# First tokens projected without their LayerNorm, the factors multiplied in behind: an attention and MLP kernel on one Trainium2 core

## The chip, the cores and the metric

The kernel runs on one core of one Trainium2 chip. The metric is the device time of one execution in microseconds; the time of a kernel is the median of its runs.

## What is computed

One input `x` (2048 tokens of 512) goes through a LayerNorm without parameters, and the result `xn` feeds two branches that meet at the end:

```python
def _layernorm(x, axis=-1, eps=1e-5):
    m = jnp.mean(x, axis=axis, keepdims=True)
    v = jnp.var(x, axis=axis, keepdims=True)
    return (x - m) / jnp.sqrt(v + eps)

xn = _layernorm(x)
# attention: 32 heads of 128, 2048 cached keys and values, no mask
q = (xn @ wq).reshape(B, Sq, H, Dh).transpose(0, 2, 1, 3)
p = softmax(einsum("bhqd,bhkd->bhqk", q, k_cache) * Dh ** -0.5)
s = einsum("bhqk,bhkd->bhqd", p, v_cache).transpose(...).reshape(B, Sq, H * Dh) @ wo
# MLP: 512 -> 512 (gelu), shifted by tokens in four column groups, -> 512; then 512 -> 1792 -> 512
x1 = xn + shift(gelu(layernorm(xn) @ w1)) @ w2
g = silu(x1 + gelu(layernorm(x1) @ w3) @ w4)
out = x + s * g
```

Inputs are bf16.

## The kernel before

Attention is cut into 128 units. A unit is one head and 512 queries; units go by groups of four heads, and within a group by the four blocks of 512 queries, so units 0 to 3 are the first 512 tokens with heads 0 to 3, units 4 to 7 the next 512 tokens. A unit has 8 steps (`SPU`), 1024 in all; the loop over `n` in the main function writes out the order of the work by hand, step by step, and `pin` keeps each engine's instructions in that order. A step does, on TensorE, two score matmuls (`s_slot`: 128 keys by 512 queries each, into one of two PSUM buffers `ps_s`), one exp of both on ScalarE, and the two PV matmuls of an earlier step (`pv_slot`, into a bank of `psO`, which has two). The distance between a step's scores and its PV is the lag: `LAG` at first, one more behind each entry of `STEPS`. So before the change the lag is 5 up to step 35, 6 up to 39, 7 up to 43, 8 up to 47, and in the long run 10 to 12.

Everything else is woven in between. VectorE adds up the exps of a unit (`add_first`, `add_next`, `fold`, all of the tile `acc`); the row sums come out of matmuls with a column of ones for units 0 to 3 (`sums`) and out of a DMA transpose for the later ones; the reciprocals go to DRAM and come back broadcast over the partitions (`recip`, `bcast`: DMAs on SP's queue), and `norm` multiplies them into the PV result, which frees its PSUM bank. The query projection of a unit is four matmuls (`q_mm`) and a copy (`q_copy`). MLP chunks are dealt out evenly from step 42 on, into the PSUM bank with the tag `xm`; the other bank of the pool `psX`, tag `xa`, serves queries, sums and output projection in turn.

LayerNorm of x goes by tiles of 128 tokens: `ln1_load`, `ln1_stats` (`bn_stats`, `bn_aggr` on VectorE, the reciprocal root as two small GpSimd instructions), `ln1_apply` (VectorE), `ln1_turn` (a DMA transpose into `xnT`). The tuple `tokens` gives the steps at which tiles 4 to 15 do so. Tiles 0 to 3 are handled before step 0, by `first_stats` and `first_tokens`: normalise, transpose on TensorE against an identity matrix, copy to `xnT`, project unit 0's query in four pieces of 128 tokens. Units 1 to 3 get their queries at steps 1, 3 and 5, four matmuls at a time. Before all that, `warm_up` runs 48 small matmuls on the identity. Loads are issued on three queues: SP (`nc.sync`), ScalarE's (`nc.scalar`) and GpSimd's (`nc.gpsimd`); `load_k`, `load_v` and `load_w` fetch a head's K (transposing, in four pieces), V (two halves) and query weights.

Helpers record every matmul at one line (L122), so groups are told apart by their tiles: `ps_s` scores, `ps_o` PV, `ps_q` queries, `ps_m` MLP, `ps_wo` output projection, `ps_sum` row sums.

## Time and profile before

| | us |
|---|---|
| median of 3 runs | 1249.71 |
| lowest and highest | 1249.54, 1253.06 |
| profiled execution | 1248.59 |
| its span, first to last instruction | 1246.8 |
| TensorE busy | 1239.2 |
| ScalarE busy | 1129.5 |
| VectorE busy | 1115.2 |
| GpSimd busy | 171.3 |

The profile is of one execution. A row of its timeline gives the start, the length, the engine, the line, the operation with its output and inputs, the number of instructions merged, and in brackets the idle time of the engine ahead of it and what ended that. A row of a group gives the number of instructions behind an x, the busy time, the mean of one in ns, and the idle time ahead of them. PE is TensorE's matmuls and PEld its weight loads, DVE VectorE, ACT ScalarE, POOL GpSimd, SP SyncE; a trailing q is the engine's DMA queue. Matmuls overlap, so the sum of their durations is more than the time they take: their pace is read from starts.

### The profile page before, as it was taken

Reading aid. Unit: us, or ns where it says so; the run is one execution under the profiler, and the core shown is the slowest. Engines: PE = TensorE matmul, PEld = TensorE weight load, DVE = VectorE, ACT = ScalarE, POOL = GpSimd, SP = SyncE. Lnnn points to the kernel's source line nnn. Section 1 sums busy time; section 2 is a strip of 40 time slices with the busy share of each in tenths; the row PEclk is TensorE's granted clock in tenths of the full one; section 3 lists DMA queues with packets and bytes.
Section 4 is the critical chain, followed back from the end, with each engine's and each line's share of the span. In section 5 each row is a group of like instructions: output and inputs, shape, how many; then the busy total and the mean of one; then the engine's idle time right before and its main releaser. Section 6 shows DMA issues by size and latency. Waiting matters only on the chain.

```text
span 1246.8 us, 16616 instructions
## 1 busy us (share of the span) xinstructions
PE 1239.2 (99%) x5808; PEld 596.4 (48%) x5808; DVE 1115.2 (89%) x1518; ACT 1129.5 (91%) x1285; POOL 171.3 (14%) x299
## 2 busy tenths in 40 slices
PE   8999999999999999999999999999999999999998
PEld 5444444444444444444444444444444444444444
DVE  7999999999899988899989889899888999888998
ACT  8999999888999888899998889998888999988992
POOL 5563003432111000000100000010000000000110
PEclk9999999999999999999999999999999999999999
DMA  9556473565734545243573345633345233653453
GB/s 198 126 111 104 88 154 77 129 130 114 153 67 101 114 98 120 55 88 73 108 155 85 68 76 106 136 79 83 81 105 119 56 89 66 130 136 77 106 149 106
DMA packets 248404, 131.42 MB, mean 105 GB/s; under 512 B 200000, under 2 KB 224960, under 8 KB 248320
## 3 DMA queue, kind: packets, MB, share of 16 engines
q1 hardware_dynamic: 238752, 103.94, 41.1%
q0 software_dynamic: 8992, 25.96, 8.0%
q8 instruction: 45, 0.74, 0.3%
q10 hardware_dynamic: 576, 0.46, 0.1%
q14 instruction: 39, 0.32, 0.1%
HBM read 83.62 MB, written 8.13 MB: 74 GB/s over the span
## 4 chain that ended last, share of the span: by engine, by line
PE 93%; DVE 3%; DMA 2%; ACT 1%; issue 0%; SPq 0%; DVEq 0%
PE ps_s L122 34%; PE ps_o L122 33%; PE ps_m L122 9%; PE ps_wo L122 8%; PE ps_q L122 8%; DMA rb<-dr 1%; DVE acc L224 1%; ACT pT L213 1%; DMA dr<-rc 0%; DVE acc L219 0%; DMA accT<-acc 0%; DVE qT L199 0%; DVE sm L266 0%; DVE acc L228 0%; DVE oT L293 0%
## 5 line engine op out<-in xcount | busy, mean ns | idle before, releaser
L213 ACT ACTIVATE pT<-ps_s 128x1024 bf16<-128x1024 f32 x1024 | 1022.1, 1029 | 90.7 <-PE ps_s L122 76.3
L122 PE MATMUL ps_s<-qT,kT 128*128 128x512 bf16 x2048 | 608.8, 379 | 0.8 <-ACT pT L213 0.5
L122 PE MATMUL ps_o<-pT,vb 128*128 128x512 bf16 x2048 | 607.4, 379 | 0.4 <-DVE oT L300 0.4
L122 PEld LDWEIGHTS <-kT 128*128 128x128 bf16 x2048 | 231.7, 113 | 228.8 <-issue 6.0
L224 DVE TENSOR_TENSOR acc<-acc,pT 128x2048 bf16<-128x2048 bf16 x256 | 308.9, 1207 | 7.3 <-ACT pT L213 6.6
L122 PEld LDWEIGHTS <-vb 128*128 128x128 bf16 x2048 | 200.2, 98 | 226.0 <-issue 0.7
L219 DVE TENSOR_TENSOR acc<-pT 128x2048 bf16<-128x2048 bf16 x128 | 156.2, 1221 | 30.9 <-ACT pT L213 30.5
L122 PE MATMUL ps_q<-xnT,wq_h 128*128 128x512 bf16 (+1 forms) x524 | 152.8, 374 | 0.6 <-ACT xnT L477 0.4
L293 DVE TENSOR_TENSOR oT<-ps_o,rb 128x512 bf16<-128x512 f32 x122 | 130.8, 1072 | 9.5 <-DMA rb<-dr 9.4
L122 PE MATMUL ps_wo<-wo_h,oT 128*128 128x512 bf16 (+1 forms) x460 | 135.1, 377 | 0.0
L379 DVE TENSOR_TENSOR s_acc<-ps_wo,s_acc 128x512 f32<-128x512 f32 x96 | 66.0, 688 | 42.6 <-PE ps_wo L122 42.4
L228 DVE TENSOR_TENSOR acc<-acc 128x1024 bf16<-128x1024 bf16 x128 | 87.5, 683 | 0.9
L266 DVE TENSOR_REDUCE sm<-accT 128x4 f32<-128x512 bf16 x122 | 83.0, 680 | 1.1 <-DMA accT<-acc 1.0
L199 DVE CAST qT<-ps_q 128x512 bf16<-128x512 f32 x109 | 75.0, 688 | 7.9 <-PE ps_q L122 6.9
L122 PEld LDWEIGHTS <-wq_h 128*128 128x128 bf16 x524 | 50.8, 98 | 60.8 <-issue 1.0
L122 PE MATMUL ps_m<-w_sb,h2T 128*128 128x512 bf16 x224 | 77.1, 379 | 0.5 <-DVE xr L700 0.5
L122 PE MATMUL ps_m<-xn2T,w_sb 128*128 128x512 bf16 x224 | 77.1, 379 | 0.0
L682 POOL DMA_DIRECT2D w_sb<-in_B_w_dram x28 | 21.2, 756 | 372.3 <-PE ps_m L122 325.3
L122 PEld LDWEIGHTS <-oT 128*128 128x128 bf16 x468 | 45.7, 98 | 54.1
L710 POOL DMA_DIRECT2D g_d<-xr x16 | 8.8, 548 | 438.3 <-DVE xr L708 438.3
L229 DVE TENSOR_TENSOR acc<-acc 128x512 bf16<-128x512 bf16 x128 | 54.4, 425 | 4.4
L514 DVE SCALAR_TENSOR_TENSOR sq<-sq,pre 128x1024 bf16<-128x1024 bf16 x36 | 44.0, 1222 | 4.7 <-ACT sq L510 4.6
(98 smaller groups left out, 627.9 us busy)
## 6 DMA issues: line engine op xcount, KB each, us to landing
rb<-dr SPq DMA_DIRECT2D x127, 256.0 KB, 3.9
vb<-in_A_v_cache_dram SPq DMA_DIRECT2D x60, 256.0 KB, 3.4
w_sb<-in_B_w_dram POOLq DMA_DIRECT2D x28, 256.0 KB, 3.6
wo_h<-in_A_wo_dram SPq DMA_DIRECT2D x32, 128.0 KB, 2.8
wq_h<-in_A_wq_dram SPq DMA_DIRECT2D x28, 128.0 KB, 2.9
kT<-in_A_k_cache_dram SPq DMA_TRANSPOSE x128, 3.4
dr<-rc SPq DMA_DIRECT2D x128, 2.0 KB, 1.7
xr<-in_A_x_dram POOLq DMA_DIRECT2D x16, 128.0 KB, 2.5
```

The lines of the kernel that those rows point to most:

```text
L122: pin(nc.tensor.matmul(out=out, lhsT=lhsT, rhs=rhs, start=start, stop=stop))
L199: pin(nc.vector.tensor_copy(out=qT[:], in_=st[u].pop("psq")[:]))
L213: pin(nc.scalar.activation(out=s["pT"][-1][:, jj:jj + 2, :], in_=sps[:], func=ACT.Exp, scale=SCALE))
L219: pin(nc.vector.tensor_tensor(out=s["acc"][:], in0=s["pT"][0][:], in1=s["pT"][1][:], op=ALU.add))
L224: pin(nc.vector.tensor_tensor(out=a[:], in0=a[:], in1=st[u]["pT"][i][:], op=ALU.add))
L228: pin(nc.vector.tensor_tensor(out=a[:, 0:2, :], in0=a[:, 0:2, :], in1=a[:, 2:4, :], op=ALU.add))
L229: pin(nc.vector.tensor_tensor(out=a[:, 0, :], in0=a[:, 0, :], in1=a[:, 1, :], op=ALU.add))
L266: pin(nc.vector.tensor_reduce(out=sm[:], in_=s.pop("at")[:], axis=mybir.AxisListType.X, op=ALU.add))
L293: pin(nc.vector.tensor_tensor(out=oTs[(g, qt)][:, hh, :].rearrange(f, j=4), in0=s["o"].rearrange(f, j=4), in1=s["rb"].rearrange("x (p j) - ...
L379: pin(nc.vector.tensor_tensor(out=sa, in0=ps[:], in1=sa, op=ALU.add))
L514: pin(nc.vector.scalar_tensor_tensor(out=sq[:].rearrange(f2), in0=sq[:].rearrange(f2), scalar=1.0, in1=pre[:].rearrange(f2), op0=ALU.add, ...
L682: pin(nc.gpsimd.dma_start(out=w[:], in_=w3_v[:, :, fc * P:(fc + 2) * P]))
```

## The change

The change has three parts.

First, the four tiles of the first 512 tokens are no longer normalised before they are projected. `first_tokens` transposes the raw x on TensorE (`turn`, `back`) into a tile `xT`. The mean is taken out on the side of the weights: `middle` multiplies a head's query weights with a matrix of -1/512, copies the result (`cs`) to SBUF, and GpSimd adds it to the weights in one instruction per head (`wc`), so that the projection of raw x by `wc` is that of x less its mean. The reciprocal roots of the variances come behind: `factor` spreads them over the partitions with fp32 matmuls against a diagonal matrix (`rsA` broadcast, `diag`), and `q_scale` multiplies them into the projected queries on VectorE. `first_stats` takes all four tiles on VectorE and one root of four columns on GpSimd. The query matmuls of units 1 to 3 become single ones and pairs: two ahead of step 0, two each at steps 0, 1, 2 and 15, one each at 9 and 12 (`raw_q`, `raw_fill`). Tiles 0 to 3 are still normalised for the MLP, tile 0 ahead of step 0 and the others at steps 0 and 1, and are transposed by DMA at steps 34, 40, 46 and 52. Tiles 8 to 15 have other steps in `tokens`.

Second, the third unit (`u == 2`) gathers its PV in the bank `xm`, and the normalisations of units 0 to 3 move from steps 18, 26, 34, 42 to 26, 34, 38, 42; broadcasts 1 and 3 have other SBUF buffers. The queries of units 4 to 6 use the bank `xa`, those of 5 and 6 in two pairs instead of four singles.

Third, the lag starts at 3 and grows to 4, 5 and 6 behind steps 15, 23 and 32, and is as before from step 36 on. The warm-up has 23 matmuls on the -1/512 matrix, with 4 more ahead of the query projection. x tiles 0 to 3 are all loaded on SP's queue, the first two query weights on ScalarE's; unit 0's V halves stand between its K pieces; the loads of tiles 4 to 7 move ahead, and V of the second head moves from ahead of step 0 to steps 2 and 4, that of the third from steps 3 and 4 to 7 and 8, all on GpSimd's queue.

```diff
-    LAG = 5
+    LAG = 3
-    WARM = 48
+    WARM = 23
+    FILL = 4
...
-    STEPS = (36, 40, 44, 48, 49, 150, 158)
+    STEPS = (15, 23, 32, 40, 44, 48, 49, 150, 158)
...
+            s["o"] = (psX.tile([P, 512], FP32, tag="xm", name="ps_o") if u == 2 else
+                      psO.tile([P, 512], FP32, name="ps_o"))
...
     def first_stats():
...
+        ve = smp.tile([P, 4], FP32, tag="rc", name="ve4")
+        for a in range(2):
+            bns = [smp.tile([P, nc.vector.BN_STATS_DIM], FP32, name="bn") for _ in range(2)]
+            for j in range(2):
+                pin(nc.vector.bn_stats(out=bns[j][:], in_=ln[2 * a + j][:]))
+            for j in range(2):
+                pin(nc.vector.bn_aggr(out=mvA[:, 2 * a + j, :], in_=bns[j][:]))
+        pin(nc.vector.tensor_scalar(
+            out=ve[:], in0=mvA[:, :, 1], scalar1=EPS, scalar2=None, op0=ALU.add))
+        return lambda: pin(nc.gpsimd.tensor_tensor(
+            out=rsA[:], in0=ve[:], in1=nhalf[:, 0:1].to_broadcast([P, 4]), op=ALU.pow))
...
+    def q_raw(h, dcs, ps, cs=slice(0, 512)):
+        for dc in dcs:
+            mm(ps[:, cs], raw[h][:, dc, :], raw["xT"][:, dc, cs], dc == 0, dc == DC - 1)
+
+    def q_scale(h, ps, rb, cs=slice(0, 512)):
+        if h not in st:
+            st[h] = dict(qT=qtp.tile([P, 512], BF16, name="qT"))
+        pin(nc.vector.tensor_tensor(out=st[h]["qT"][:, cs], in0=ps, in1=rb, op=ALU.mult))
...
     def first_tokens():
...
+        def factor(i):
+            rp_ = psO.tile([P, 256], FP32, tag="ps_o", name="ps_r")
+            for j in range(2):
+                t = 2 * i + j
+                mm(rp_[:, j * P:(j + 1) * P], rsA[:, t:t + 1].to_broadcast([P, P]), diag[:], True, True)
+            return rp_
+
+        tok = lambda t: slice(t * P, (t + 1) * P)
+        roots = first_stats()
+        for t in range(2):
+            turn(t)
+            back(t)
+        middle((0,), psX.tile([P, P], FP32, tag="xa", name="ps_c"))
+        for t in range(2, 4):
+            turn(t)
+            back(t)
+        roots()
+        middle((1,), psO.tile([P, P], FP32, tag="ps_o", name="ps_c"))
+        warm_up(FILL, psX.tile([P, P], FP32, tag="xm", name="ps_w"))
+        ps = [psX.tile([P, 512], FP32, tag=tag, name="ps_q") for tag in ("xa", "xm")]
+        for i in range(2):
+            for t in (2 * i, 2 * i + 1):
+                q_raw(0, range(DC), ps[i], tok(t))
+            pin(nc.scalar.activation(out=qs[:, halves[i]], in_=ps[i][:, halves[i]], func=ACT.Identity))
+        rps = [factor(i) for i in range(2)]
+        ln1_apply(0)
+        for i in range(2):
+            q_scale(0, rps[i][:], qs[:, halves[i]], halves[i])
+        middle((2,), psX.tile([P, P], FP32, tag="xm", name="ps_c"))
+        for i in range(2):
+            pin(nc.scalar.activation(out=rsb[:, halves[i]], in_=rps[i][:], func=ACT.Identity))
+
+    def middle(hs, cp, eng=None):
+        c = slice(hs[0] * P, hs[0] * P + P)
+        for h in hs:
+            for dc in range(DC):
+                mm(cp[:], raw["mean"][:], wqs[h][:, dc, :], dc == 0, dc == DC - 1)
...
+        for h in hs:
+            wide(h)
+            pin(nc.gpsimd.tensor_tensor(
+                out=raw[h], in0=wqs[h][:], in1=raw["cs"][:, h * P:(h + 1) * P].unsqueeze(1).broadcast_to([P, DC, P]),
+                op=ALU.add))
...
-    for t, eng in enumerate([nc.sync, nc.scalar, nc.sync, nc.scalar]):
+    for h in range(2):
+        load_w(h, nc.scalar)
+    for t, eng in enumerate([nc.sync] * 4):
         ln1_load(t, eng)
+    for i in range(2):
+        load_k(0, (2 * i, 2 * i + 1))
+        load_v(0, (i,))
+    raw_q = {-1: [(1, 0), (1, 1)], 0: [(1, 2), (1, 3)], 1: [(2, 0), (2, 1)], 2: [(2, 2), (2, 3)],
+             9: [(3, 0)], 12: [(3, 1)], 15: [(3, 2), (3, 3)]}
...
     first_tokens()
-    load_v(1, (0, 1), nc.gpsimd)
...
-        at(3 + i, lambda i=i: load_v(2, (i,), nc.gpsimd))
+        at(2 + 2 * i, lambda i=i: load_v(1, (i,), nc.gpsimd))
+        at(7 + i, lambda i=i: load_v(2, (i,), nc.gpsimd))
...
+    norms = {26: 0, 34: 1, 38: 2, 42: 3}
...
+    scales = {2: 1, 5: 2, 15: 3}
+    raw_fill(-1)
     for n in range(NS):
...
-        if u == 0 and p in (1, 3, 5):
-            q_mm(1 + p // 2, range(DC))
-        if u == 0 and p in (2, 4, 6):
-            q_copy(p // 2)
+        if n == 2:
+            middle((3,), psO.tile([P, P], FP32, tag="ps_o", name="ps_c"), nc.vector)
+        raw_fill(n)
+        if n in scales:
+            h = scales[n]
+            q_scale(h, raw["ps", h][:], raw["rb"][:])
+        if n in (0, 1):
+            for t in (2 * n, 2 * n + 1)[n == 0:]:
+                ln1_apply(t)
+        if n in (34, 40, 46, 52):
+            ln1_turn((n - 34) // 6)
...
+        if n in norms:
+            normed(norms[n])
-        if p == 2 and u >= 2 and not turned(u - 2):
+        if p == 2 and u > HG + 1 and not turned(u - 2):
             normed(u - 2)
```

More of the change, by code (lines that the diff above doesn't have):

```diff
@@ L496, in first_tokens, with back @@
[L496 to L499 removed]
+                mm(tps[t].rearrange(f, c=DC)[:, dc, :], ln[t][:, dc * P:(dc + 1) * P], ident[:], True, True)
+        def back(t):
+            pin(nc.scalar.activation(out=xT[:, :, t * P:(t + 1) * P], in_=tps[t].rearrange(f, c=DC), func=ACT.Identity))
```

142 lines of the change are left out of this document (53 added, 89 removed).

## The prediction

> **What bounds the kernel now.** I read the page first: its busy times and the engine shares of the chain that ended last.
>
> ```profile
> PE 1239.2 (99%) x5808; PEld 596.4 (48%) x5808; DVE 1115.2 (89%) x1518; ACT 1129.5 (91%) x1285; POOL 171.3 (14%) x299
> PE 93%; DVE 3%; DMA 2%; ACT 1%; issue 0%; SPq 0%; DVEq 0%
> ```
>
> TensorE sets the end. So the question is where it loses time, and the change touches the start only: in program order TensorE's list is the same in both kernels from step 39 on (a step is one pair of score matmuls, 1024 in all), VectorE's from the eighth unit on. The view by stretches, cut at the first score matmul (10.04 us), at step 22's (31.24) and at step 44's (54.22):
>
> ```profile
> 0.00:10.04 10.04, 7.12 (x80) 6.18 (x81) 5.24 (x16) 5.26 (x11) 8.33 (x19) 1.00 0.95 166
> 10.04:31.24 21.20, 20.53 (x98) 9.69 (x98) 16.74 (x29) 20.10 (x22) 8.25 (x15) 1.00 0.96 213
> 31.24:54.22 22.98, 22.98 (x113) 11.10 (x112) 21.84 (x37) 21.55 (x23) 13.91 (x26) 1.00 0.67 150
> 100.00:660.00 560.00, 560.00 (x2595) 268.09 (x2594) 509.24 (x688) 519.93 (x599) 75.78 (x125) 1.00 0.52 108
> ```
>
> After the length the columns are TensorE's busy time and count, weight loads, VectorE, ScalarE, GpSimd, clock, DMA share, GB/s. The last row gives the pitch of a 512-column matmul in a full stream: 560/2595 = 0.216 us. The TensorE groups of the second stretch:
>
> ```profile
> L122 PE MATMUL ps_s<-qT,kT 128*128 128x512 bf16 x44 | 12.8, 378 | 0.7 <-ACT qT L499 0.4 <-ACT pT L213 0.3
> L122 PE MATMUL ps_o<-pT,vb 128*128 128x512 bf16 x34 | 10.1, 378 | 0.4 <-DVE oT L300 0.4
> L122 PE MATMUL ps_q<-xnT,wq_h 128*128 128x512 bf16 x12 | 3.1, 379 | 0.0
> L122 PE MATMUL ps_sum<-ones_t,acc 128*128 128x1 bf16 x8 | 0.5, 170 | 0.0
> ```
>
> 44+34+12 = 90 wide matmuls x 0.216 = 19.4 us, and some 0.3 for the eight narrow ones: 19.7 of 21.2, so **1.5 us are lost in steps 0 to 21**. In the third stretch 105 wide ones (113 less 8 sums) need 22.7+0.3 = 23.0 of 22.98: nothing is lost. Gain can come from those 1.5 us and from the 10.04 us ahead of the first score.
>
> The timeline of the start, and its two losses at steps 6 and 21:
>
> ```profile
> 1.36 2.43 POOL L179 DMA_DIRECT2D wq_h<-in_A_wq_dram  x3 [0.29 <-issue]
> 3.31 0.69 DVE L417 BATCH_NORM_STATS2 bn<-xin 128x6 f32<-128x512 bf16 x1 [1.98 <-DMA xin<-in_A_x_dram]
> 4.62 0.57 POOL L423 TENSOR_TENSOR rsA<-ve,nhalf 128x1 f32<-128x1 f32 x1
> 6.34 0.82 POOL L423 TENSOR_TENSOR rsA<-ve,nhalf 128x2 f32<-128x2 f32 x1
> 6.60 1.09 ACT L477 ACTIVATE xnT<-ps_o 128x512 bf16<-128x512 f32 x2 [0.67 <-PE ps_o L122]
> 7.67 0.40 PE L122 MATMUL ps_s<-ident,xn 128*128 128x128 bf16 x4
> 7.95 2.16 POOL L396 DMA_DIRECT2D xin<-in_A_x_dram  x4
> 8.60 0.38 ACT L494 ACTIVATE qT<-ps_q 128x256 bf16<-128x256 f32 x1
> 9.17 0.29 DVE L496 CAST qT<-ps_q 128x128 bf16<-128x128 f32 x1
> 9.71 0.28 ACT L499 ACTIVATE qT<-ps_q 128x128 bf16<-128x128 f32 x1 [0.74 <-PE ps_q L122]
> 10.04 1.03 PE L122 MATMUL ps_s<-qT,kT 128*128 128x512 bf16 x4 [0.36 <-ACT qT L499]
> 10.67 5.85 ACT L213 ACTIVATE pT<-ps_s 128x1024 bf16<-128x1024 f32 x6 [0.68 <-PE ps_s L122]
> 16.85 13.85 ACT L213 ACTIVATE pT<-ps_s 128x1024 bf16<-128x1024 f32 x15 [0.33 <-PE ps_s L122]
> 30.07 0.69 DVE L300 TENSOR_TENSOR oT<-ps_o,rb 128x512 bf16<-128x512 f32 x1 [1.51 <-DMA rb<-dr]
> ```
>
> ScalarE needs 0.91 us per exp when it is never starved ((13.85-1.0)/14), TensorE 0.86 for two scores and two PVs: the two are nearly tied, so where the query matmuls and PVs lie decides who waits. The 30.07 row is the other loss: unit 0's normalisation waits for its broadcast, and unit 2's PV waits for unit 0's PSUM bank (the 0.4 in the ps_o group).
>
> **Steps 0 to 21 after the change.** Lag 3 (4 from step 15) gives TensorE its first PV at step 3 instead of 5; the 12 query matmuls of units 1 to 3 are spread (two ahead of step 0, then two each at steps 0, 1, 2, 15 and one at 9 and 12) instead of three lumps of four; unit 2 has a bank of its own. By step 22 the list holds 44 scores, 36 PVs, 10 query matmuls, 4 small ones for unit 3's column means (0.2 us) and 8 sums: 19.4+0.2+0.3 = 19.9 us. ScalarE's bound on step 22 is exp 20's end (two score buffers): 0.63 to the first exp, 20 x 0.91, and 1.03: 19.9 too. So the loss of 1.5 can all but vanish; I keep 0.2 for steps in which one or the other leads. The list is then two wide matmuls (0.43) ahead, since two query matmuls fell before step 0. Sum: -1.5 + 0.2 + 0.2 - 0.43 = **-1.5 us**, if no new wait comes.
>
> **VectorE as cover.** Its groups up to 60 us:
>
> ```profile
> L224 DVE TENSOR_TENSOR acc<-acc,pT 128x2048 bf16<-128x2048 bf16 x12 | 14.6, 1213 | 0.7 <-ACT pT L213 0.6
> L402 DVE BATCH_NORM_STATS2 bn<-xin 128x6 f32<-128x512 bf16 x10 | 6.8, 683 | 0.0
> L199 DVE CAST qT<-ps_q 128x512 bf16<-128x512 f32 x7 | 4.8, 684 | 3.3 <-PE ps_q L122 3.1
> L429 DVE TENSOR_SCALAR xn<-xin,mv,rs 128x512 bf16<-128x512 bf16 x9 | 3.6, 402 | 0.0
> L228 DVE TENSOR_TENSOR acc<-acc 128x1024 bf16<-128x1024 bf16 x5 | 3.5, 690 | 0.1
> L229 DVE TENSOR_TENSOR acc<-acc 128x512 bf16<-128x512 bf16 x5 | 2.1, 425 | 0.2
> ```
>
> It loses nothing by scaling (three 0.68 casts become multiplies of the same shape), but takes three normalisations of the first tokens (3 x 0.40) into steps 0 and 1 and one copy (0.29). Up to unit 0's sums at step 11 it has five normalisations 2.0, three statistics 2.0 and their aggregates about 0.5, the copy 0.3, two scalings 1.4, three additions 3.6 and the folds 1.1: 10.9 us, where TensorE reaches the sums about 10.8 after step 0. No slack, no debt: 0 to 0.3 us, and it coincides with the wait for V below. The later norms (steps 26, 34, 38, 42) only free banks that are wanted after: unit 3's PV starts at 29, the MLP takes unit 2's bank at 42. The four extra transposes on SP's queue fall at steps 34 to 52, each ahead of its MLP chunk.
>
> **The start.** ScalarE's back-copies cost what they did (1.09 for two). New are GpSimd's four adds of the column mean to a weight tile (128x512, two inputs), the four fp32 matmuls that spread the factors, and a longer queue on GpSimd. Rows for those:
>
> ```profile
> 0.83 0.24 POOL L82 IOTA diag<- 128x128 f32 x1 [0.40 <-POOLq L992]
> 14.45 1.50 POOL L174 DMA_DIRECT2D vb<-in_A_v_cache_dram  x2
> 23.27 1.19 DVE L219 TENSOR_TENSOR acc<-pT 128x2048 bf16<-128x2048 bf16 x1
> 23.44 1.10 POOL L126 TENSOR_SCALAR ve<-mv 128x1 f32<-128x1 f32 x1 [0.25 <-DVE mv L403]
> vb<-in_A_v_cache_dram POOLq DMA_DIRECT2D x4, 256.0 KB, 6.9
> wq_h<-in_A_wq_dram SPq DMA_DIRECT2D x28, 128.0 KB, 2.9
> ```
>
> No row has such an add. The iota writes 128 elements in 0.24: one stream of 512 costs at least 4 x 0.24 = 0.95; three streams one after the other 2.9. The two reads are likelier to share a path than the write: 1.2 us, near the low end. The Trainium skill (GPSIMD Engine Reference, Performance versus the Vector engine) gives 4497 ns for such an add of 2048 fp32 elements, a quarter of which is an estimated 1.1; nothing else here rests on it.
>
> The chain: x0 lands at 3.3 (VectorE's first row), the others 0.4 to 0.5 apart on one queue, the first weight (ScalarE's queue, 2.9) by 4. Two transposes (0.40 each) and back-copies (0.55) end by 5.1, unit 0's means are copied (0.28) by 5.4, where GpSimd's issues end too (1.36 + 2 x 0.81 + 2.16 = 5.1). Add 0: to 6.6. The root of four columns: 0.57 for one and 0.82 for two make about 1.3 for four: to 7.9. Add 1: to 9.1. Unit 0's 16 small matmuls end by 7.7, their copies (2 x 0.38) by 8.4, in the shadow. The fp32 factor matmuls have no row: 0.06 each as bf16 ones, 0.6 each if four passes each load weights anew; 0.3, as the matmul is short and its operand wide: 9.1, latency 0.2, VectorE's second half-scaling 0.4 (between 0.29 for 128 and 0.68 for 512 columns): 9.7. The other way, add 1 and two query matmuls, ends at 9.5. With 0.1 for each of three handovers **step 0 starts at 10.0**, as before: 0, between -0.8 and +1.4.
>
> **SP's queue at the start** takes all four x loads and then unit 0's K pieces, with a V half behind each two:
>
> ```profile
> 1.65 5.12 SPq L164 DMA_TRANSPOSE kT<-in_A_k_cache_dram  x4
> kT<-in_A_k_cache_dram SPq DMA_TRANSPOSE x16, 5.5
> ```
>
> Two more x issues put the first piece 0.9 later, at 2.5; with 5.5 to landing it is there at 8.0, ahead of step 0. The third is issued near 5.7 and lands at 11.2, wanted at step 4 (13.7). Hidden; a K 2 us later than that would begin to cost.
>
> **Two new waits.** The query matmuls of unit 2 at step 1 wait for add 2, which follows unit 2's means: about 11.3 to 12 against TensorE's 11.3: 0.2 (0 to 0.7). And unit 1's V: its issue moves on GpSimd's queue from 10.1 behind add 2, add 3 and the statistics of tokens 4 and 5, about 5.3 to 6.2 us after step 0, since the small rows can be held while VectorE adds (the 23.44 row lasts 1.10 inside the 23.27 row). It landed 6.9 after its issue under full queues, where SP's queue gave other loads 2.9; unit 1's first PV stands at step 11, 10.4 after step 0. At 2.9 nothing waits, at 6.9 some 2 to 3 us. There is less in flight beside it than before: I take 5.3, a wait of 0.6, and keep 0 to 3.0. Behind it on TensorE stand step 12's scores, so ScalarE starves too.
>
> **Sum.** -1.5 + 0 + 0.2 + 0.6 = -0.7 us. The profiled execution took 1248.59 (its span 1246.8 and 1.8 around it), so 1247.9; the median of the runs shown is 1.1 above it: **1249.0 us**.
>
> **Rivals.**
> - *V lands late (0.20).* For: the 6.9 row. Against: it is the median of a busier stretch. Wait 3.0 instead of 0.6: 1251.4.
> - *The adds cost the dear end (0.12), the slower side.* 2.9 each on GpSimd, because three streams serialise or VectorE holds it off. Add 0 ends at 8.3, root 9.6, add 1 at 12.5, step 0 at 13.0 (+3.0); add 2 is 1.2 late at step 1; V follows two more of them, 3 us late at step 11. -1.5+3.0+1.2+3.0 = +5.7: 1255.4. It turns slower than before from about 1.8 us per add.
> - *The clock stays low (0.10).* The warm-up in two halves:
>
> ```profile
> 1.39:4.55 3.16, 3.16 (x30) 3.16 (x31) 0.00 (x0) 1.00 0.95 243
> 4.55:5.73 1.18, 1.17 (x21) 1.00 (x18) 0.00 (x0) 1.00 0.92 88
> ```
>
> 30 matmuls took 0.105 each, then the rest 0.056 (18 weight loads in 1.00), though the clock column says 1.00 all along. Now 23 warm-up matmuls are over by about 3.5, before that point, and x sets the rest. If the fast pace came only after step 0, some 40 small matmuls cost 0.05 more each, and early scores double for a microsecond or two: +2.5, 1251.5. The Trainium skill (TensorE: Matmul & The Clock Gate, Part 1) says a free-running window of about 3.4 us of activity opens the gate; the 3.16 us here agrees, and by it gaps for x in that window could keep it shut.
> - *No new wait at all (0.10).* Step 0 at 9.2, V in time: -1.5-0.8 = -2.3: 1247.4.
>
> The forecast itself has 0.48.
>
> **Range and chances.** The forecast's own bounds give 1247.4 to 1251; the range reaches to the dear rival's near half: 1246.6 to 1253.2. A measurement of this kernel can tell about 0.3% (3.7 us) from no change: faster than 1246.0 needs more than every loss there is (0.04); above 1253.5 lies most of the dear rival and a late V with a low clock (0.12); the rest, 0.84.
>
> **What would show it.** First score near 10.0; step 22's score 20 to 21 us after it; no PV waiting on oT at 30; GpSimd's adds near 1.2; a TensorE gap at step 11 with the V load behind it. A first score after 11.5, adds over 1.8, or new gaps after step 22 would make it wrong.

## The result, and the profile after

| | before | after |
|---|---|---|
| median, us (22 runs each, in turn on one chip) | 1251.36 | 1254.41 |
| lowest to highest | 1248.69 to 1256.11 | 1250.58 to 1258.59 |
| profiled execution, its span | 1248.59, 1246.8 | 1256.94, 1255.2 |

The ratio is 1.0023, with a 95% interval of 1.0013 to 1.0033: by the medians the change costs 3.05 us, where 0.7 of gain was forecast. The forecast time was 1249.0, and 1254.41 lies above its range. Of the 5.4 us between the two, 1.65 come from before, which ran at 1251.36 here and at 1249.71 in the three runs that the forecast started from; the other 3.75 lie between the gain of 0.7 and the loss of 3.05.

The profiled execution of after is 2.5 us above its median, that of before 2.8 below its own, so the two profiles lie further apart than the kernels do. Half of the distance of their spans arises behind step 500. Of that half, 2.07 us are lost in steps 520 to 545, where VectorE waits longer for broadcasts than in before (9.3 against 5.3 us over steps 515 to 565). Among the other executions below some lose nothing there (e1, which is the same kernel, e2, e6, e11, e18) and the rest 0.1 to 2.2; this is not explained, and all that lies behind step 500 is left out here. Up to there all comparisons go by the start of ScalarE's exponentials (`pT<-ps_s`, one per step). Against before, after is 3.06 us late at exponential 0, 2.59 at 22, 3.18 at 44, 3.19 at 60, 3.89 at 76 and 3.98 at 500. So **three things are to be explained: the start, steps 22 to 44, and 0.7 us between 60 and 76.**

The page of after: TensorE's busy time, and the shares of the chain that ended last. (Some of its matmul records are missing, so a step's scores are found here by the exponential behind them, not by counting.)

```profile
PE 1235.8 (98%) x5697; PEld 597.3 (48%) x5811; DVE 1117.5 (89%) x1523; ACT 1129.7 (90%) x1287; POOL 174.9 (14%) x296
PE 83%; DVE 9%; DMA 4%; ACT 2%; issue 1%; POOL 1%; SPq 0%; DVEq 0%; ACTq 0%
```

TensorE still sets the end, but more of the chain runs through VectorE and through DMAs than before (93% PE). The same stretches as in the prediction, cut at the scores of steps 0, 22 and 44:

```profile
0.00:13.11 13.11, 8.62 (x80) 7.73 (x82) 6.16 (x18) 5.30 (x12) 7.57 (x14) 0.87 0.99 193
13.11:33.74 20.63, 20.52 (x101) 9.69 (x102) 19.44 (x34) 20.33 (x24) 12.88 (x18) 1.00 0.84 168
33.74:57.42 23.68, 22.87 (x110) 10.73 (x111) 21.48 (x35) 21.48 (x23) 15.78 (x27) 1.00 0.73 152
```

The start takes 13.11 instead of 10.04, the second stretch 20.63 instead of 21.20, the third 23.68 instead of 22.98. The timeline of the start says why:

```profile
5.70 1.16 POOL L527 TENSOR_TENSOR wc<-wq_h,cs 128x512 bf16<-128x512 bf16 x1 [0.54 <-ACT cs L522]
5.92 0.69 DVE L421 BATCH_NORM_STATS2 bn<-xin 128x6 f32<-128x512 bf16 x1 [0.64 <-DMA xin<-in_A_x_dram]
8.54 0.61 PE L128 MATMUL ps_s<-ident,xin 128*128 128x128 bf16 x4 [2.19 <-DMA xin<-in_A_x_dram]
9.71 1.04 POOL L426 TENSOR_TENSOR rsA<-ve,nhalf 128x4 f32<-128x4 f32 x1 [2.85 <-DVE ve L424]
9.79 1.78 PE L128 MATMUL ps_q<-xT,wc 128*128 128x128 bf16 x16
11.41 1.11 PE L128 MATMUL ps_r<-diag,rsA 128*128 128x128 f32 x8
12.19 0.86 DVE L465 TENSOR_TENSOR qT<-ps_r,qs 128x256 bf16<-128x256 f32 x2 [0.15 <-PE ps_r L128]
13.11 0.59 PE L128 MATMUL ps_s<-qT,kT 128*128 128x512 bf16 x2
```

The third tile of x is there at 5.92 and the fourth at 8.52, not at 4.7. TensorE stands still for 2.19 us for it, and then is slow: the 16 small query matmuls take 1.78 us, 0.11 each. The add (1.16), the root (1.04) and the factors (1.11) cost what was forecast.

The waits behind step 22, in the timeline:

```profile
34.97 0.59 PE L128 MATMUL ps_q<-xnT,wq_h 128*128 128x512 bf16 x2 [0.20 <-DVE xn L430]
42.84 0.61 PE L128 MATMUL ps_o<-pT,vb 128*128 128x512 bf16 x2 [0.36 <-DMA vb<-in_A_v_cache_dram]
85.20 0.69 DVE L412 BATCH_NORM_STATS2 bn<-xin 128x6 f32<-128x512 bf16 x1
86.03 0.66 DVE L205 CAST qT<-ps_q 128x512 bf16<-128x512 f32 x1
86.74 0.59 PE L128 MATMUL ps_wo<-wo_h,oT 128*128 128x512 bf16 x2 [0.53 <-DVE qT L205]
```

At step 22 unit 4's first query matmuls wait (the row names VectorE; what they wait for shows in e4 below), at step 29 unit 3's first PV waits for its V, and at step 68 the output projection waits for a query's eviction out of the bank `xa`, ahead of which VectorE took tile 15's statistics. SP's queue before, and then after:

```profile
20.00 1.23 SPq L445 DMA_TRANSPOSE xnT<-xn  x1
25.82 0.52 SPq L283 DMA_DIRECT2D rb<-dr  x1
26.44 2.53 SPq L445 DMA_TRANSPOSE xnT<-xn  x2
33.06 0.94 SPq L174 DMA_DIRECT2D vb<-in_A_v_cache_dram  x2
```

```profile
20.49 1.22 SPq L447 DMA_TRANSPOSE xnT<-xin  x1
25.74 0.52 SPq L260 DMA_DIRECT2D dr<-rc  x1
30.78 0.34 SPq L292 DMA_DIRECT2D rb<-dr  x1
31.23 1.22 SPq L447 DMA_TRANSPOSE xnT<-xin  x1
36.64 0.32 SPq L292 DMA_DIRECT2D rb<-dr  x1
38.33 1.08 SPq L180 DMA_DIRECT2D vb<-in_A_v_cache_dram  x2
```

The last of the four row transposes (tile 7, of which unit 4's query is made) goes out at 31.23 instead of 27.7, since the broadcast `rb` ahead of it waits for `dr` to land; unit 3's V goes out at 38.33 instead of 33.06, behind the next broadcast and tile 8's transpose. And they land later. Groups of DMA issues with their median time to landing, before (15 to 50 us) and after (18 to 53 us):

```profile
xnT<-xn SPq DMA_TRANSPOSE x7, 3.3
dr<-rc SPq DMA_DIRECT2D x4, 2.0 KB, 1.9
```

```profile
xnT<-xin SPq DMA_TRANSPOSE x4, 3.9
dr<-rc SPq DMA_DIRECT2D x4, 2.0 KB, 3.5
```

### The profile page after: what moved, and what is told of

The parts are those of the page before. It is cut to its first block, busy times and chain, and to the rows that moved or that the text cites. A ratio compares the mean times of both kernels' runs of the same rounds, so it can differ in the third digit from the quotient of the medians.

```text
span 1255.2 us, 16518 instructions
## 1 busy us (share of the span) xinstructions
PE 1235.8 (98%) x5697; PEld 597.3 (48%) x5811; DVE 1117.5 (89%) x1523; ACT 1129.7 (90%) x1287; POOL 174.9 (14%) x296
## 4 chain that ended last, share of the span: by engine, by line
PE 83%; DVE 9%; DMA 4%; ACT 2%; issue 1%; POOL 1%; SPq 0%; DVEq 0%; ACTq 0%
PE ps_o L128 30%; PE ps_s L128 29%; PE ps_m L128 9%; PE ps_q L128 7%; PE ps_wo L128 7%; DVE acc L230 2%; DMA rb<-dr 1%; DVE oT L302 1%; ACT pT L219 1%; DMA dr<-rc 1%; DVE acc L225 1%; DMA accT<-acc 1%; DVE sm L273 1%; DVE acc L234 1%; DMA xin<-in_A_x_dram 1%
## 5 line engine op out<-in xcount | busy, mean ns | idle before, releaser
L128 PE MATMUL ps_s<-qT,kT 128*128 128x512 bf16 x1986 | 595.8, 379 | 1.7
L128 PE MATMUL ps_q<-xnT,wq_h 128*128 128x512 bf16 x490 | 146.2, 379 | 0.8 <-DVE xn L430 0.2
```

Source lines behind the costliest of these rows:

```text
L128: pin(nc.tensor.matmul(out=out, lhsT=lhsT, rhs=rhs, start=start, stop=stop))
```

## The experiments

The theories: **A**, tiles 2 and 3 are late because too much is loaded at once, and the later waits follow from SP's order and from the V loads that were moved; **B**, the late start alone is the loss; **C**, tile 15's statistics make the stop at step 68; **E**, an earlier start is given back, because transfers further on run by their own clock. These four letters are used in the text; an expectation that speaks of theories A to D has letters of its own. In the table, "late" is the start of that exponential against before's profiled execution, in us. The ratio is to before on the same chip. Each row of "late" is one profiled execution, and shows where time goes rather than how much on average: the profiled executions of e3, e7, e8, e10 and e15 are the slowest of their kernel's runs, those of e11, e16 and e18 the fastest.

| | first score | late at 0 | at 22 | at 44 | at 76 | ratio, 95% |
|---|---|---|---|---|---|---|
| before | 10.04 | | | | | |
| after | 13.11 | 3.06 | 2.59 | 3.18 | 3.89 | 1.0023 (1.0013 to 1.0033) |
| e1 | 12.15 | 2.10 | 1.64 | 2.95 | 3.65 | 1.0029 (1.0016 to 1.0042) |
| e2 | 15.27 | 5.22 | 4.75 | 5.18 | 5.88 | 1.0047 (1.0031 to 1.0063) |
| e3 | 11.07 | 1.02 | 0.60 | 4.38 | 5.09 | 1.0045 (1.0030 to 1.0060) |
| e4 | 10.98 | 0.94 | 0.51 | 2.18 | 2.88 | 1.0024 (1.0007 to 1.0041) |
| e5 | 11.28 | 1.23 | 0.80 | 2.76 | 3.47 | 1.0026 (1.0014 to 1.0038) |
| e6 | 10.54 | 0.49 | 0.05 | 2.82 | 3.54 | 1.0026 (1.0012 to 1.0040) |
| e7 | 10.54 | 0.49 | 0.05 | 6.78 | 7.49 | 1.0037 (1.0024 to 1.0051) |
| e8 | 10.62 | 0.58 | 0.36 | 5.28 | 6.00 | 1.0034 (1.0025 to 1.0043) |
| e9 | 11.41 | 1.37 | 0.91 | 1.88 | 2.58 | 1.0025 (1.0015 to 1.0035) |
| e10 | 14.38 | 4.34 | 3.72 | 3.29 | 4.00 | 1.0016 (1.0006 to 1.0025) |
| e11 | 11.30 | 1.25 | 0.81 | 2.17 | 3.02 | 1.0025 (1.0015 to 1.0035) |
| e12 | 10.63 | 0.58 | 0.04 | 0.69 | 2.92 | 1.0022 (1.0013 to 1.0032) |
| e13 | 10.54 | 0.49 | -0.04 | -0.30 | 0.47 | 1.0006 (0.9995 to 1.0017) |
| e14 | 11.14 | 1.09 | 0.55 | 0.31 | 1.08 | 1.0019 (1.0010 to 1.0028) |
| e15 | 11.47 | 1.43 | 1.18 | 2.83 | 3.24 | 1.0010 (1.0000 to 1.0021) |
| e16 | 9.83 | -0.21 | 0.57 | 0.78 | 1.18 | 1.0024 (1.0013 to 1.0034) |
| e17 | 10.44 | 0.39 | 0.15 | 0.31 | 0.34 | 0.9996 (0.9987 to 1.0006) |
| e18 | 9.64 | -0.40 | 1.06 | 0.84 | 0.86 | 1.0012 (1.0001 to 1.0023) |

### The start: e1 to e4

**e1**, the changed kernel unaltered:

> The changed kernel once more, unaltered. If the late arrival of the third and fourth x tile (5.9 and 8.5 us in the profile after) belongs to the change, they come at 5.5 or later again and the first score starts at 12 to 14 us, about 3 us slower than before. If it was an accident of that execution, they come by 5 and the first score starts near 10.

First score at 12.15, ratio as in the table: the start itself varies by 1 us between these two executions. The fourth tile (tile 3) landed at 7.2 instead of 8.5.

**e2**, x on two queues, the first two weights behind it on ScalarE's:

```diff
+    for t, eng in enumerate([nc.sync, nc.scalar, nc.sync, nc.scalar]):
+        ln1_load(t, eng)
     for h in range(2):
         load_w(h, nc.scalar)
-    for t, eng in enumerate([nc.sync] * 4):
-        ln1_load(t, eng)
```

> The four x tiles of the start go on SP's and ScalarE's queue in turn, as before the change, with the two query weights behind them on ScalarE's. Theory A (the weights' 256-byte pieces on ScalarE's queue take the DMA engines from x) and theory C (four x loads in a row on one queue, the last issued at 2.1 us): x is there by 4.6, first score at 10 to 10.5, about 2.5 us faster than the changed kernel. Theory B (GpSimd's early loads of tiles 4 to 7 get in front of x): x3 still after 6, first score after 11.5.

All four tiles landed by 4.8, but the first weight came at 8.0, where TensorE has it at 4.99 in e13. This is TensorE's row for the column means:

```profile
8.00 0.58 PE L128 MATMUL ps_c<-wq_h,mean 128*128 128x128 bf16 x4 [3.76 <-DMA wq_h<-in_A_wq_dram]
```

The forecast gain failed: putting x first delayed the weight. The Trainium skill (Trainium Kernel Development and Optimization, Key Constraints) says that DMAs issued from SP, ScalarE and GpSimd run on the same 16 DMA engines and interleave; this row fits that.

**e3**, tiles 4 to 7 loaded on SP behind K instead of on GpSimd; **e4**, the first two weights on GpSimd's queue ahead of the others:

```diff
# e3
     for i in range(2):
         load_k(0, (2 * i, 2 * i + 1))
+        for t in (4 + 2 * i, 5 + 2 * i):
+            ln1_load(t, nc.sync)
         load_v(0, (i,))
-    for t in range(4, 8):
-        ln1_load(t, nc.gpsimd)
# e4
-    for h in range(2):
-        load_w(h, nc.scalar)
-    for h in range(2, HG):
+    for h in range(HG):
         load_w(h, nc.gpsimd)
```

> Only the loads of x tiles 4 to 7 move, from GpSimd's queue to SP's, behind unit 0's first K pieces. Theory B: x3 lands by 5.5 and the first score starts at 10 to 11. Theories A and C: x3 lands after 6 as in the changed kernel, first score at 12 or later.

> Only the first two query weights move, from ScalarE's queue back to GpSimd's ahead of tiles 4 to 7. Theory A: x is there by 5, and the first score then waits for weight 0 and the add: 11 to 12. Theory C: x3 still after 6. Theory B: x3 lands near 6 to 7, since GpSimd's loads of tiles 4 to 7 are issued 1.6 us later.

Both start at 11.0 to 11.1, 1 us before e1, and gain nothing by it: e3 is later at exponential 44 than after, e4 as slow in the ratio. The earlier start itself proves little. The unaltered start is also in e5 and e8 to e11, and its first scores lie between 10.62 (e8) and 14.38 (e10), with tile 3 landing between 6.2 and 8.5. Of the two edits only e4 has its landing outside that spread, at 5.2 (e3: 6.5). In both TensorE stops at step 22, and here the view of waits names it, for e3 with 2.8 us, for e4 with:

```profile
PE ps_q L128 <- DMA xnT<-xin: 1.9, 1, 1.9
```

It is tile 7's transpose. Theory B falls: half of e1's late start went and the ratio did not follow, and over all rows a start at 14.38 (e10) comes with 3.29 at exponential 44 and one at 10.62 (e8) with 5.28, though these two also alter later steps.

### Single edits behind the start: e5 to e11

**e5** issues unit 0's broadcast at step 15 instead of 12, behind tile 7's transpose (at 14):

```diff
-        if p == (5 if u > T1 else 4) and u >= 1 and not turned(u - 1):
+        if p == (5 if u > T1 else 7 if u == 1 else 4) and u >= 1 and not turned(u - 1):
             bcast(u - 1)
```

> Unit 0's broadcast load moves from step 12 to step 15, so that on SP's queue the transposes of token tiles 6 and 7 no longer stand behind it and its wait for the reciprocals' trip to DRAM. Theory (the queries of unit 4 at step 22 wait for tile 7's transpose, because of that order): the transpose is issued about 2 us earlier and the wait ahead of step 22's query matmuls (0.4 to 3.0 us in the runs so far) goes; exp 0 to exp 44 takes about 44.0 us instead of 44.4 to 47.8. Rival (the transpose is late because the DMA engines are full then): it lands as late as before and the wait stays. The start stays as in the changed kernel, first score at 12 to 13.

The wait at step 22 is gone (0.80 late at exponential 22, 0.27 at 24) and the time is there all the same: the next transfer on the queue is now late.

```profile
PE ps_o L128 <- DMA vb<-in_A_v_cache_dram: 1.5, 1, 1.5
```

**e6** holds back loads at the start: x1 on ScalarE's queue, tiles 4 to 7 on SP behind K, and an instruction on GpSimd that reads tile 2 ahead of its loads. **e7** is e5 and e6 together; **e8** is the changed kernel with the old lags.

```diff
# e6, beside e3's lines
+    for t, eng in enumerate([nc.sync, nc.scalar, nc.sync, nc.sync]):
+        ln1_load(t, eng)
     for h in range(2):
         load_w(h, nc.scalar)
-    for t, eng in enumerate([nc.sync] * 4):
-        ln1_load(t, eng)
+    held = smp.tile([P, 1], FP32, tag="ve", name="held")
+    pin(nc.gpsimd.tensor_scalar(out=held[:], in0=ln[2][:, 0:1], scalar1=EPS, scalar2=None, op0=ALU.add))
# e8
-    LAG = 3
+    LAG = 5
-    STEPS = (15, 23, 32, 40, 44, 48, 49, 150, 158)
+    STEPS = (36, 40, 44, 48, 49, 150, 158)
```

> The start's loads in another order: x0, x2, x3 on SP's queue, x1 and the first two weights on ScalarE's, x tiles 4 to 7 behind unit 0's K pieces on SP's queue, and a small GpSimd instruction that reads x2 ahead of GpSimd's own loads, so that these start only when x2 is there. Theory (x is late because more is in flight than the DMA engines can move): x3 by 5, first score at 10.1 to 10.5, time 2 to 2.5 us below the changed kernel. Rival (the late x3 is one straggling DMA engine, whatever else is in flight): x3 at 6 or later, first score at 11 or later.

> The last two together. If both theories hold, the first score is at 10.1 to 10.5, no wait at step 22, and the time is 3 to 4 us below the changed kernel and within 1 us of the kernel before. If only one holds, the gain is that one's.

> The changed kernel with the lags of before (5 up to step 35). The prediction's step (the lag of 3 takes most of the 1.5 us out of steps 0 to 21): exp 0 to exp 22 takes 21.2 us as before the change, against 20.74, and one PV pair (0.43) less is done by then. Rival (the spread query matmuls and the third bank did it, not the lag): 20.7 or less, so the time differs from the changed kernel's by under 0.5 us.

e6 mends the start (0.49 late) and is level with before at exponential 22 (0.05); by 44 it is 2.82 late, to waits of 1.7 for the transpose and 1.3 for V. e7 waits 3.3 for V alone, and loses more behind that wait (the last section has it). The lags are not the cause of the stop: e8 has it too, at step 22, with 2.9 us. What the lags are worth lies between the two expectations: from exponential 0 to 22 e8 takes 20.98, before 21.21 and after 20.74, one execution each. Theory E is now the leading one.

**e9** loads V of units 1 and 2 where it was before; **e10** puts tiles 8 and 9 back to steps 27 and 31, so that unit 3's V goes ahead of them on SP; **e11** puts tiles 12 to 15 back to the old steps.

```diff
# e9
     first_tokens()
+    load_v(1, (0, 1), nc.gpsimd)
-        at(2 + 2 * i, lambda i=i: load_v(1, (i,), nc.gpsimd))
-        at(7 + i, lambda i=i: load_v(2, (i,), nc.gpsimd))
+        at(3 + i, lambda i=i: load_v(2, (i,), nc.gpsimd))
# e10
-              (16, 20, 20), (21, 25, 25),
+              (21, 27, 27), (26, 31, 31),
# e11
-              (49, 55, 55), (55, 61, 61), (60, 66, 66), (65, 70, 70))
+              (37, 45, 45), (47, 53, 53), (55, 61, 61), (63, 69, 69))
```

> V of units 1 and 2 is loaded where it was before (unit 1 behind the first tokens, unit 2 at steps 3 and 4), all else as changed. Theory A (those transfers, 1 MB that now runs from 19 to 28 us, slow the small ones on SP's queue: the store of unit 0's reciprocals lands after 4.3 us instead of 1.7, the row transposes after 3.9 instead of 2.9): both land as before, the wait for tile 7's columns at step 22 is gone, and exponential 0 to 44 takes 43.0 to 43.8 us instead of 44.5 to 45.3; time 1251 to 1252. Theory B (SP's order alone, the broadcast ahead of the transpose): landings and waits stay, 44.5 or more, time 1252.5 to 1253.5. Theory D (the two loads then collide with the K pieces and tokens earlier, at steps 3 to 11): new gaps in steps 3 to 12, exponential 0 to 22 over 21.2 us.

> Tiles 8 and 9 are normalised and transposed at the old steps (27 and 31 instead of 20 and 25), so that V of unit 3 stands ahead of tile 8's transpose on SP's queue. Theory A: V of unit 3 is issued 1.3 us earlier, the wait of unit 3's first PV at step 29 (0.3 to 1.6 us) goes, the one at step 22 stays; time 0.3 to 1 us under the changed kernel's 1252.5. Theory B (V is late because of the broadcast of unit 1 ahead of it): gain under 0.3.

> Tiles 12 to 15 are taken at the old steps (45, 53, 61, 69 instead of 55, 61, 66, 70). Theory C (the step of 0.7 us that every run so far loses at step 68 is the statistics of tile 15 ahead of the eviction of unit 10's query on VectorE, for which the output projection's bank waits): the gap of 0.70 us at step 68 goes, exponential 60 to 76 takes 23.6 instead of 24.3 us, time 0.7 under the changed kernel's 1252.5. Rival: the gap stays (the eviction is late by the lags), or comes at another step.

e9: the V loads were not what slows the others; a wait of 1.2 stays at step 22. e10 has no wait for V any more, as its own theory A said, and it shows what is possible: 43.35 us from exponential 0 to 44, where before takes 44.40. But its start came at 14.38. With a start that late, tile 7's columns are in time too. e11 removes the stop at step 68 (theory C holds: 0.01 us lost between 60 and 76), and a new one of 0.7 comes at step 45 for an output weight.

### Combinations: e12 to e18

**e12** is e5, e6, e9, e10 and e11 together:

> The three edits above, with the loads held at the start (step 0 at 10.5) and unit 0's broadcast at step 15. If each part of the loss has the cause named (start 0.5 to 1.2 us above before's, 1.5 to 2.8 lost in steps 22 to 30 to late transfers, 0.7 at step 68): exponential 44 at most 0.5 us later than before's, exponential 76 too, time 1249.0 to 1250.5, ratio 0.999 to 1.001. If an earlier start is only given back (theory E: some chain on SP's queue that does not move with the start sets steps 22 to 44): a wait comes back in steps 22 to 44, exponential 44 is 2 us or more later than before's, time 1252 or more.

```profile
PE ps_wo L128 <- DMA wo_h<-in_A_wo_dram: 1.9, 2, 1.5
PE ps_o L128 <- DMA vb<-in_A_v_cache_dram: 1.0, 1, 1.0
```

Step 22 is free; two transfers further on are late. **e13** is e12 with unit 3's V taken off SP's queue, and with tiles 12 to 15 as in the changed kernel but for tile 15's statistics, which stand at step 63:

```diff
-              (37, 45, 45), (47, 53, 53), (55, 61, 61), (63, 69, 69))
+              (49, 55, 55), (55, 61, 61), (60, 66, 66), (63, 70, 70))
-    ... (20, load_v, 3, 0), (22, load_v, 3, 1)
+        at(13 + 2 * i, lambda i=i: load_v(3, (i,), nc.gpsimd))
```

> The combined version (loads held at the start, unit 0's broadcast at step 15, V of units 1 and 2 early, tiles 8 and 9 at steps 27 and 31), with V of unit 3 loaded from GpSimd's queue at steps 13 and 15 instead of SP's at 20 and 22, and of tiles 12 to 15 only the last one's statistics at step 63 instead of 65. If the four causes are all (start, late transposes at step 22, late V at step 29, VectorE at step 68): no gap in steps 22 to 30, none at 45 or 68; exponential 0 to 44 takes 43.2 to 43.5 us against before's 44.4, exponential 76 comes 0.3 to 0.7 us earlier than before's, time 1248.8 to 1249.8, ratio 0.9985 to 1.000. Theory E (an earlier start is given back): a new wait of 0.5 to 1.5 us in steps 20 to 46, exponential 76 0.5 to 2 us later than before's, time 1250.5 to 1252.

No transfer is late up to step 62: exponential 44 comes 0.30 us before that of before, 43.61 after exponential 0. The ratio is 1.0006 (0.9995 to 1.0017), so **the loss is gone, and no gain is left either.** One stop is left, of theory C's kind at another place: the statistics at step 63 now stand ahead of unit 5's normalisation, for whose bank unit 7's PV waits.

```profile
79.64 1.04 DVE L302 TENSOR_TENSOR oT<-ps_o,rb 128x512 bf16<-128x512 f32 x1
80.73 0.59 PE L128 MATMUL ps_o<-pT,vb 128*128 128x512 bf16 x2 [0.59 <-DVE oT L302]
```

The next three build on e13. **e14** shortens the start by two roots of two columns, the first ahead of the adds on GpSimd; **e15** is e13 with the first tile's normalisation behind the scalings of the query, and tile 15's statistics at step 67; **e16** is e15 with the third and fourth weight on SP's queue.

```diff
# e14
-        roots = first_stats()
+    first_stats(0)()                     # ahead of GpSimd's loads
+        roots = first_stats(1)
+        rps = [factor(0)]
         middle((1,), ...)
...
-        rps = [factor(i) for i in range(2)]
+        rps.append(factor(1))
# e15
-              (63, 70, 70))
+              (67, 71, 71))
-        ln1_apply(0)
         for i in range(2):
             q_scale(0, rps[i][:], qs[:, halves[i]], halves[i])
+        ln1_apply(0)
# e16
-    held = ...
-    for h in range(2, HG):
-        load_w(h, nc.gpsimd)
     for i in range(2):
         load_k(0, (2 * i, 2 * i + 1))
+        for j in range(2):
+            load_w(2 + j) if i == 0 else ln1_load(4 + j, nc.sync)
         load_v(0, (i,))
...
     first_tokens()
+    for t in (6, 7):
+        ln1_load(t, nc.gpsimd)
```

> As e13, and the root of the four first tiles is taken in two halves of two columns: the first ahead of the centred weights on GpSimd, its factor matmuls ahead of the query matmuls on TensorE. If the chain behind the centred weights (root 1.05, factor matmuls 1.16, first scaling 0.4) sets the start: the first score comes 0.6 to 1.0 us earlier (9.6 to 10.0 instead of 10.6), exponential 76 0.9 to 1.7 us earlier than before's, time 1247.9 to 1249.0, ratio 0.998 to 0.9995. If the landing of the third and fourth tile or of the first weight sets it: no change against e13. If the earlier start is given back: the first score is earlier and exponential 76 is not.

> As e13, with the first tile's normalisation behind the two scalings of unit 0's query on VectorE instead of ahead of them, and tile 15's statistics at step 67 (its normalisation and transpose at 71). In e13 that normalisation took 1.25 us beside the second centred-weight addition on GpSimd and ended as the first scaling began. Theory A (it is on the path): first score 0.3 to 0.5 us earlier (10.1 to 10.25), the stop of 0.75 at step 66 gone and no other in its place, exponential 76 0.3 to 0.8 us earlier than before's, time 0.8 to 1.2 under e13's on the same chip, ratio 0.9985 to 1.0000. Rival: the factor matmuls (end 9.75) set the scaling as well, the first score stays at 10.4 to 10.6; or the gain is given back by a wait in steps 20 to 70.

> As e15, with the third and fourth weight issued from SP's queue behind the first two pieces of K instead of from GpSimd, where their issue (1.72 us) ended just as the first centred-weight addition began, 0.3 us after its input; tiles 4 and 5 follow on SP, 6 and 7 on GpSimd behind the additions. If GpSimd's issue work holds the addition: it starts at 5.9 instead of 6.2, the first score at 9.8 to 9.95, exponential 76 0.6 to 1.1 us earlier than before's, ratio 0.998 to 0.9995. If the landing of the first weight or the third and fourth tile sets it: as e15. If the later tiles 4 to 7 or K pieces are late: a new wait in steps 0 to 16.

e14 missed: the first root pushed GpSimd's weight loads to 5.91 and these the first add to 7.65 (6.19 in e13).

```profile
5.91 1.73 POOL L185 DMA_DIRECT2D wq_h<-in_A_wq_dram  x2
7.65 1.17 POOL L527 TENSOR_TENSOR wc<-wq_h,cs 128x512 bf16<-128x512 bf16 x1
```

e15 is inconclusive on its first point, since the query matmuls ran at half pace again (first score 11.47). Its profiled execution is the slowest of its eleven, and shows what one landing can do: tile 7's transpose was issued at 28.84 (28.64 in e13) and landed after 6.2 us (3.3 in e13), hence again

```profile
PE ps_q L128 <- DMA xnT<-xin: 1.9, 1, 1.9
```

e16 starts at 9.83, ahead of before, and is late again by exponential 22: 0.5 at the transpose and

```profile
PE ps_sum L128 <- DVE acc L235: 1.3, 1, 1.3
```

unit 0's sums at step 11, for which VectorE is late: it had waited 0.45 for a root on GpSimd, and the normalisation behind that took 1.25 beside GpSimd's add, where others take 0.40.

**e17** is e15 with K of unit 3 behind tile 7's transpose, and tile 15's statistics at step 52; **e18** is that with e16's start and tiles 6 and 7 on SP:

```diff
# e17
-    (8, load_k, 3, 0), (11, load_k, 3, 1), (15, load_k, 3, 2), (19, load_k, 3, 3)
+    (15, load_k, 3, 0), (16, load_k, 3, 1), (17, load_k, 3, 2), (19, load_k, 3, 3)
-              (67, 71, 71))
+              (52, 70, 70))
# e18, beside e16's first lines: behind unit 0's K and V
+    for t in (6, 7):
+        ln1_load(t, nc.sync)
```

> As e15, with K of unit 3 loaded at steps 15 to 19 (behind tile 7's transpose at step 14 on SP's queue) instead of 8 to 19, and tile 15's statistics at step 52 (its normalisation and transpose at 70). If SP's queue, which runs by its own clock, makes tile 7's columns late: its transpose is issued at 25.5 to 27 us instead of 28.6 to 28.8, no wait at step 22 for any start between 10 and 11.5, no stop at steps 66 to 82 beyond before's 0.32, exponential 0 to 44 takes 43.0 to 43.6 us, ratio 0.9985 to 1.0005. If the landing (2.4 to 6.2 us) decides: a wait of 0.5 or more at step 22 again, 44.5 or more. If K of unit 3 becomes late: a wait at step 24.

> As e17, with the third and fourth weight on SP's queue as in e16, tiles 6 and 7 on SP too, so that GpSimd has the additions and V alone. If GpSimd's queue made e16 wait 1.5 us at step 11: that wait falls to under 0.5, first score at 9.8 to 10, exponential 0 to 44 43.0 to 43.8 us, exponential 76 0.8 to 1.4 us earlier than before's, ratio 0.998 to 0.9995. If an earlier start is given back on VectorE or SP whatever the queue: waits of 1 us or more in steps 8 to 30 and a time no better than e17's.

In e17 the transposes of tiles 6 and 7 do go out earlier, and land no earlier; SP's row, the landing, and the wait that is left:

```profile
25.42 2.60 SPq L447 DMA_TRANSPOSE xnT<-xin  x2
xnT<-xin SPq DMA_TRANSPOSE x2, 6.1
PE ps_q L128 <- DMA xnT<-xin: 0.4, 1, 0.4
```

There is no stop between exponential 44 and 76 any more (0.31 and 0.34 late). Its median is 1250.14 against 1251.00, and the ratio, which is not taken from the medians, is 0.9996 (0.9987 to 1.0006): level with before. e18 has the earliest start of all, 9.64, and loses it at step 8, as unit 1's K is not there:

```profile
19.21 0.62 PE L128 MATMUL ps_s<-qT,kT 128*128 128x512 bf16 x2 [2.13 <-DMA kT<-in_A_k_cache_dram]
```

while the DMA engines, by the view by stretches, are busy all the time:

```profile
10.00:20.00 10.00, 7.87 (x40) 3.64 (x38) 9.90 (x17) 7.82 (x10) 8.50 (x11) 1.00 1.01 211
```

That is theory E: **in the profiles of e18, e16, e17 and e13, starts of 9.6, 9.8, 10.4 and 10.5 us all reach exponential 44 between 0.3 us ahead of before and 0.8 behind it.** In e18 a late K takes the early start back, which is what theory E says; in e16 it is mostly VectorE, with 1.3 of the 1.8 us waited. No version beats the kernel before.

What the ratios show by themselves is less than what the traces show. None of e2 to e12 brought the ratio clear of that of after. e17, which puts several edits together, did, and e13 nearly (its interval and that of after share 1.0013 to 1.0017): the loss is in the parts that they mend. How it divides among these parts is read from single executions.

## Why the prediction was wrong, point by point

Two terms that the sum put at nothing failed: the start, and what lies behind step 22. By exponentials, steps 0 to 21 were to bring 0.7 us and brought 0.47 in after and 0.46 in e1. The start cost 3.06 and 2.10 instead of 0. Steps 22 to 76 cost 1.30 and 2.01 instead of 0. Two of the signs that the prediction named for being wrong came: a first score after 11.5, and new gaps after step 22.

- **The start (0, between -0.8 and +1.4): wrong by 3.1 in the profiled execution, through one term.** Add 1.16 (forecast 1.2), root 1.04 (1.3), four factor matmuls 1.11 (1.2). What failed is the first sentence of the chain, "the others 0.4 to 0.5 apart on one queue": tiles 2 and 3 landed at 5.9 and 8.5. That spacing is of issues, not of landings. My own quoted row had the DMA engines at 0.95 of their time in this stretch, and the change put more into it (0.99). Where the loads were held back, tile 3 landed at 5.2 to 5.6 and the same chain started at 10.4 to 10.6 (e6, e7, e12, e13, e17; e15, at half pace, at 11.5), and at 9.6 to 9.8 with GpSimd free (e16, e18). The size of 3.1 is partly chance: of the seven executions with this start, four began at 10.6 to 11.4, inside the forecast's bounds (e5, e8, e9, e11), and three outside (after, e1, e10).
- **Rival "the clock stays low": came, in after through the stop for tile 3,** not through the warm-up: 16 query matmuls in 1.78 instead of the 1.07 of e13, 0.7 us of the start. In e9, e11 and e15 it came much as forecast: the small matmuls did not leave half pace before about 10 us, though none of their stops ahead of the query was longer than 0.9. The 16 query matmuls of e9, and below them those of e5, whose stops (0.4 and 1.1) were no shorter:

```profile
7.77 1.91 PE L128 MATMUL ps_q<-xT,wc 128*128 128x128 bf16 x16
7.75 1.06 PE L128 MATMUL ps_q<-xT,wc 128*128 128x128 bf16 x16
```

- **Rival "the adds are dear": no.** 1.16 each.
- **V of unit 1 (0.6 of wait, up to 3.0): no wait.** Its halves landed after 3.4 us. VectorE's bound at step 11, "no slack, no debt", was right (0.14 us in after), and it bit when the start came earlier (e16).
- **Steps 0 to 21 (-1.5 + 0.2 + 0.2, and 0.43 ahead): mis-sized.** Cut at the scores, 0.57 us was gained instead of 1.1. The gap at unit 2's PV is gone, as said; but by the starts of its matmuls TensorE waits 0.6 us in all between a PV and the next scores, which wait for an exponential, and 0.2 ahead of sums: "0.2 for steps in which one or the other leads" was too little where the two are tied.
- **"In the third stretch nothing is lost": the step that decided whether any gain could be kept.** I took it from the profile of before and looked for new work in it, not for data that it waits for. Tile 7's transpose stands behind a broadcast that waits for a store to land (1.7 us in before, 5.0 in after for the first), and unit 3's V behind the next broadcast as well. After loses 0.70 us there by its scores, and e6 shows what waits behind a mended start: with 0.49 late at exponential 0, it loses 2.8 us there.
- **"VectorE's [list is the same] from the eighth unit on": wrong.** The statistics of tile 15 moved from step 63 to 65, ahead of a query's eviction: 0.70 us (e11 and e17, where they stand elsewhere, lose nothing between exponentials 60 and 76).

What stays open: what is lost in steps 520 to 545 in most of these executions; and what makes one transpose land after 2.4 us and the next after 6.2, with the same order on SP's queue (e13 and e15). The DMA engines are 0.81 to 1.13 busy by the view in stretches of 10 us up to 30 us (before, after, e13, e18; the view adds up the times of packets, so the share can pass 1); that their load is the cause is likely, and was not isolated.

## What to carry to other kernels

When the DMA engines are nearly full over the first stages, the time at which data arrives is the schedule: an earlier start or a removed stall is worth only what the last transfer of each later stage allows, so list the transfers that each stage needs with issue, landing and due time before counting a gain. A queue entry that waits (a broadcast behind a store) delays every entry behind it, also those that have long been ready: in after SP's queue stood from 28.84 to 30.78. An instruction moved by two steps on a full VectorE can cost its own length if an eviction stands behind it.

## What the hardware showed unexpectedly

VectorE stands still beside GpSimd. In e13, the sum of epsilon and four variances, which took 0.17 us in after, lasted 1.24, up to the end of the first add on GpSimd (6.19 + 1.17), and the first tile's normalisation 1.25 beside the second add, where the later ones take 0.40:

```profile
6.16 1.24 DVE L424 TENSOR_SCALAR ve<-mvA 128x4 f32<-128x4 f32 x1
6.19 1.17 POOL L527 TENSOR_TENSOR wc<-wq_h,cs 128x512 bf16<-128x512 bf16 x1
8.52 1.16 POOL L527 TENSOR_TENSOR wc<-wq_h,cs 128x512 bf16<-128x512 bf16 x1
8.57 1.25 DVE L430 TENSOR_SCALAR xn<-xin,mvA,rsA 128x512 bf16<-128x512 bf16 x1 [1.17 <-POOL rsA L426]
```

The Trainium skill (SBUF — State Buffer, SBUF: two separate sides) calls the port pair that the two engines share an exclusive lock, held for a whole instruction, and names the kinds of VectorE instruction that take it; the ends of the first two rows fit that (7.40 and 7.36). Whether an instruction as small as the first is of those kinds, no run here tells apart.

TensorE can fall back to half pace after a stop. In e7 it waited 3.26 us for V, and its next 15 wide matmuls took 5.94 us, 0.4 each instead of 0.216, with a granted clock of 0.53:

```profile
43.75 1.03 PE L128 MATMUL ps_o<-pT,vb 128*128 128x512 bf16 x2 [3.26 <-DMA vb<-in_A_v_cache_dram]
43.75:49.69 5.94, 5.94 (x15) 2.19 (x16) 1.23 (x1) 2.59 (x3) 2.19 (x8) 0.53 0.21 74
```

So this late transfer cost its wait and nearly as much again (15 x 0.18 = 2.7 us). The Trainium skill (TensorE: Matmul & The Clock Gate, Part 1) says that the clock goes back after an idle window of about 3.4 us; e7 comes near that. But here shorter stops in the stream were followed by half pace too: 2.8 us in e3 and 2.9 in e8, both with a granted clock of 0.50 over the next 3.4 us, and 2.19 at the start of after. Stops of 1.9 (e4, e15) and 2.1 (e18) were not.
